# Two chunks' q loaded as token pairs behind the first raw weight blocks, and transposed by 64-column products

## Chip, core and metric

The kernel runs on one core of one Trainium2 chip. The metric is the device time of one execution in microseconds (us). The kernel before took 668.18, 668.00 and 666.48 us in three runs (median 668.0). Engines are named as in the profile: PE (TensorE, with PEld for its weight loads), DVE (VectorE), ACT (ScalarE), POOL (GpSimd) and SP (SyncE, which here only issues DMAs).

## What is computed

Attention with a decay over blocks of 64 tokens, then two dense layers with `h - tanh(h)` between them. Cut to what matters:

```python
# q, k, v: (batch 4, heads 8, tokens 768, head_dim 64) float32; lam: (8,)
Dmask = where(i >= j, lam ** (i - j), 0)
for b in range(12):                       # blocks of 64 tokens
    intra = (qb @ kb.T * Dmask) @ vb
    inter = (qb * lam ** (i + 1)) @ kv_state
    out[:, :, block] = intra + inter
    kv_state = lam ** 64 * kv_state + (kb * lam ** (63 - i)).T @ vb
x = out.transpose(0, 2, 1, 3).reshape(3072, 512)
h = x @ w_in                              # 512 x 2048
result = (h - tanh(h)) @ w_out            # 2048 x 512
```

The two weight matrices arrive as 8-byte floats (`moe_w_in`, `moe_w_out`), and the kernel rounds them itself.

## The kernel before

**Chunks and groups.** The kernel works on blocks of `BLK` = 128 tokens. A chunk is one such block of one batch entry with all 8 heads; a group `g` is the four chunks (`b` = 0 to 3) of the same block, so there are 6 groups. A chunk's q, k and v are each 128 tokens x 512 numbers, 256 KB. In the first two groups (`g < GB`) they are loaded with one token on a partition by `load_natural` (L127 to L133): 8 runs of 256 bytes on each of 128 partitions. Later groups load q and k in another form that the change does not touch.

**Attention of the first group.** `att_transpose` (L323) turns q and k of a chunk so that the head dimension lies on the partitions: four PE transposes of 128x128 into a PSUM bank `tp` (L336) and one ACT copy to SBUF (L338), first for q, then for k. A transposed tile has two heads stacked in its 128 partitions and four such pairs side by side. `att_scores` (L345) makes eight products `sp` of k and q (L352), and DVE multiplies them with the decay mask into `ss` (L356). `att_decay` (L361) scales k in place. `att_state` (L363) makes the state `kv` of two chunks (L374), which ACT copies to `state` (L382). `att_out` (L384) makes the output `op` of two chunks (L406), which ACT copies to `xt` (L410). Banks of the tag `att` come from a ring of four.

**First layer.** `up_plain(u, cs)` (L731) multiplies `xt` by unit `u` of `w_in` (L741), where a unit is a quarter of the 2048 columns and comes in four blocks of 512 KB. The first blocks are loaded with 128 partitions at once (L207), the third and fourth block of each unit in two halves of 64 partitions (L210). `round_block` rounds a raw block: three ACT passes (L289, L290, L291) and two DVE passes (L294, L296). Four raw buffers exist, so a fifth block's load waits until the first has been rounded. ACT's tanh (L748) and a DVE subtraction (L749) end `up_plain`.

**What sets the order.** The work of the first group is written out by hand and kept in program order on each engine (`tied`, `keep_in_program_order`): chunks 0 and 1 are transposed and scored one after the other, then `kv` of both; then chunk 2 is transposed, the first raw block rounded, `op` of chunks 0 and 1, scores of chunk 2, the first step of `up_plain(0, (11, 21))`, chunk 3's transposes and scores between the next steps, `kv` and `op` of chunks 2 and 3, and the last steps, of which the last two pairs need the third and the fourth raw block. Behind that come `up_plain(0, (12, 22))` and the next units. What is not tied is placed by a scheduler with its own estimates.

**Loads.** SP issues the opening loads in program order (L302 to L309): q, k, v of chunk 0, q, k, v of chunk 1, q and k of chunk 2, raw blocks 0 and 1, q and k of chunk 3, raw block 2 (two halves), v of chunks 2 and 3, raw block 3 (two halves). The q pool has two buffers, so the third q waits for the transposes of the first, and the fourth for those of the second. k has three buffers, so the fourth k waits for the `kv` products of chunk 0. The whole opening is SP's one queue.

Of the kernel before, what the change touches and what calls it, by code (L numbers as in the profile page):

```python
# [9 lines left out]
F32 = mybir.dt.float32  # L10
# [5 lines left out]
AF = mybir.ActivationFunctionType  # L16
AL = mybir.AluOpType

BLK = 128
GB = 2  # L20
# [4 lines left out]
def kernel(  # L25
# [32 lines left out]
    nc = tc.nc  # L58
    B, H, S, D = q.shape
    NTOK, DM = out.shape  # L60
    DFF = moe_w_in.shape[1]
    NP = H // 2
# [12 lines left out]
    io = ctx.enter_context(tc.tile_pool(name="io", bufs=4))  # L75
    work = ctx.enter_context(tc.tile_pool(name="work", bufs=2))
# [8 lines left out]
    qpool = early.enter_context(tc.tile_pool(name="qpool", bufs=2))  # L85
# [4 lines left out]
    ident = const.tile([128, 128], F32)  # L90
# [5 lines left out]
    for j in range(2):  # L96
        for p in range(NP):
            h = 2 * p + j
# [20 lines left out]
    def tied(yes, op):  # L119
        return tc.keep_in_program_order(op) if yes else op  # L120


    raw, late = {}, {}
    chunks = [(g, b) for g in range(NG) for b in range(B)]
    at = {"loaded": 0}

    def load_natural(g, b, names):  # L127
        for name, src, bufs in (("q", q, 2), ("k", k, 3), ("v", v, 4)):
            if name in names:
                x = (qpool if name == "q" else io).tile([128, H, D], F32, name=f"{name}_nat", tag=name, bufs=bufs)  # L130
                op = nc.sync.dma_start(out=x, in_=src[b, :, ts(g, BLK), :].rearrange("h s d -> s h d"))
                tc.keep_in_program_order(op)
                raw[g, b][name] = x  # L133
# [12 lines left out]
    def load(n):  # L146

        while at["loaded"] < min(n, len(chunks)):  # L150
            g, b = chunks[at["loaded"]]
            if g < GB:
                raw[g, b] = {}
                load_natural(g, b, "qkv")
                at["loaded"] += 1
                continue
            for b in range(B):
                raw[g, b] = {}
            nat = "kv" if g < NG - 1 else "v"

            first = (0, 1, 2) if g == GB else ()
            for b in first:
                load_natural(g, b, nat)
            for b in range(B - 1):
                load_blocks(g, b, "qk")
            load_blocks(g, 3, "q")
            for b in (0, 1):
                if b not in first:
                    load_natural(g, b, nat)
            load_blocks(g, 3, "k")  # L170
            for b in (2, 3):
                if b not in first:
                    load_natural(g, b, nat)
            at["loaded"] += B
# [27 lines left out]
    def load_block(eng, dst, kind, n, m, first=False):  # L202

        if kind == "out":
            tied(n > 4, eng.dma_start(out=dst, in_=moe_w_out[ts(2 * (n + m) - n % 2, 128), :].rearrange("k (a n) -> k a n", a=2)))
        elif m < 2:
            tied(first, eng.dma_start(out=dst, in_=w_in_u[ts(m, 128), n]))  # L207
        else:
            for j in range(2):
                tied(first, eng.dma_start(out=dst[ts(1 - j, 64)], in_=w_in_u[ts(2 * m + j, 64), n]))  # L210

    def load_weights(n):

        while ready["loaded"] < min(n, len(blocks)):
            if moe_w_in.dtype != F32:
                raw64 = stage.tile([128, 2, 256], I64, name="raw64", tag="raw64", bufs=WAHEAD)
                block = blocks[ready["loaded"]]
                load_block(nc.sync if block[0] == "in" or block[1] > 4 else nc.gpsimd, raw64, *block, block[0] == "in")
                wraw[ready["loaded"]] = raw64
            ready["loaded"] += 1  # L220
# [77 lines left out]
    def bank(name, tag, bufs):  # L298
        return psum.tile([128, 512], F32, name=name, tag=tag, bufs=bufs)


    for b in range(B):  # L302
        raw[0, b] = {}
        load_natural(0, b, "qkv" if b < 2 else "qk")
        if b >= 2:
            load_weights(b if b == 2 else 3)
    for b in (2, 3):
        load_natural(0, b, "v")
    load_weights(WAHEAD)  # L309
# [10 lines left out]

    tr, sc, kdec, xt = {}, {}, {}, {}

    def att_transpose(g, bs):  # L323
        for b in bs:
            load(g * B + b + 1)
            t = raw[g, b]
            qt = work.tile([128, NP, BLK], F32, name="qt", tag="qt")
            kt = work.tile([128, NP, BLK], F32, name="kt", tag="kt")
            for dst, x in ((qt, "q"), (kt, "k")):
                if g >= GB:  # L330
                    tc.keep_in_program_order(nc.vector.transpose(out=dst.rearrange("d p i -> d (p i)"),
                                                                 in_=t[x + "b"].rearrange("d p r a -> d (p r a)")))
                else:
                    tp = bank("tp", "att", 4).rearrange("d (p s) -> d p s", p=NP)
                    for p in range(NP):
                        tied(g == 0 or p == 0, nc.tensor.transpose(out=tp[:, p, :], in_=t[x][:, 2 * p:2 * p + 2, :],  # L336
                                                                   identity=ident))
                    tied(g == 0, nc.scalar.activation(dst, tp, AF.Copy))  # L338
            qd = None
            if g > 0:  # L340
                qd = work.tile([128, NP, BLK], F32, name="qd", tag="qd")
                nc.vector.tensor_tensor(qd, qt, fwd, op=AL.mult)
            tr[g, b] = (qt, kt, qd)
# [79 lines left out]
    def attention(g):  # L423
        pieces = [[(fn, g, bs) for fn in (att_transpose, att_scores, att_out, att_state)] for bs in ((0, 1), (2, 3))]
        pieces[1].append((att_sums, g, None))
        return pieces
# [378 lines left out]
    for b in (0, 1):  # L805
        att_transpose(0, (b,))
        att_decay(0, b)
        att_scores(0, (b,))
    att_state(0, (0, 1))
    half = up_plain(0, (11, 21))  # L810
    att_transpose(0, (2,))
    att_decay(0, 2)
    weights(1)
# [149 lines left out]
```

## Time and profile before

| What | Value |
|---|---|
| Median of three runs | 668.0 us (666.48 to 668.18) |
| Profiled execution, whole time | 667.48 us |
| Its span, first to last instruction | 665.7 us |
| PE busy | 653.7 us, 98% |
| DVE, ACT, POOL busy | 480.1, 214.8, 196.4 us |
| Granted PE clock | 1.00 in all stages |
| First 30 us: DMA engines | busy from 3 us on |

The span is the time from the first to the last instruction of one profiled execution; its whole time is 1.8 us longer. The views used below are: the page (busy times by engine), lists of waits (engine and line, what it waited for, us in total, times, longest), the chain of waits (followed back from the end, each step the thing that ended last), timelines (start, length, engine and line, tiles, count), a table of busy time by stage, and the DMA view, which gives for an issue the time until its data landed. PE instructions are counted as records; a product in this kernel shows as two records, a transpose as one. A busy PE is not PE at its peak, and records may be missing by a few per cent.

### The profile page before, as it was taken

Reading aid. Unit: us, or ns where it says so; the run is one execution under the profiler, and the core shown is the slowest. Engines: PE = TensorE matmul, PEld = TensorE weight load, DVE = VectorE, ACT = ScalarE, POOL = GpSimd, SP = SyncE. Lnnn points to the kernel's source line nnn. Section 1 sums busy time; section 2 is a strip of 40 time slices with the busy share of each in tenths; the row PEclk is TensorE's granted clock in tenths of the full one; section 3 lists DMA queues with packets and bytes.
Section 4 is the critical chain, followed back from the end, with each engine's and each line's share of the span. In section 5 each row is a group of like instructions: output and inputs, shape, how many; then the busy total and the mean of one; then the engine's idle time right before and its main releaser. Section 6 shows DMA issues by size and latency. Waiting matters only on the chain.

```text
span 665.7 us, 13244 instructions
## 1 busy us (share of the span) xinstructions
PE 653.7 (98%) x4992; PEld 594.6 (89%) x4992; DVE 480.1 (72%) x869; ACT 214.8 (32%) x413; POOL 196.4 (30%) x340
## 2 busy tenths in 40 slices
PE   8899999999999999999999999999999999999988
PEld 7788888888888999888999988999988899988987
DVE  4468897997778983489895378896378787357743
ACT  4788923423321113341112343112333112334110
POOL 0001415783122444001435101345200255300351
PEclk9999999999999999999999999999999999999999
DMA  9999936997345979426889533798721677600584
GB/s 215 226 205 272 294 124 221 347 323 215 79 91 147 294 219 268 88 52 133 233 236 288 132 73 87 182 291 252 202 50 37 156 239 237 205 16 1 141 278 167
DMA packets 158959, 121.76 MB, mean 183 GB/s; under 512 B 133872, under 2 KB 135024, under 8 KB 158896
## 3 DMA queue, kind: packets, MB, share of 16 engines
q0 software_dynamic: 26400, 86.27, 40.7%
q1 hardware_dynamic: 132352, 34.64, 25.6%
q8 instruction: 40, 0.66, 0.4%
q14 instruction: 23, 0.19, 0.1%
q10 hardware_dynamic: 144, 0.00, 0.0%
HBM read 100.67 MB, written 20.19 MB: 182 GB/s over the span
## 4 chain that ended last, share of the span: by engine, by line
PE 76%; issue 9%; DVE 5%; DMA 5%; POOL 2%; ACT 2%; SPq 1%; POOLq 0%; DVEq 0%; ACTq 0%
PE y L458 14%; PE y L686 11%; PE z L458 8%; PE zw L686 8%; PE h L741 7%; PE w L633 4%; PE y L633 4%; PE y L542 3%; PE sp L352 3%; PE op L406 3%; PE acc L771 2%; PE z L542 2%; PE op L400 1%; PE end L725 1%; DMA fine<-wt 1%
## 5 line engine op out<-in xcount | busy, mean ns | idle before, releaser
L598 POOL DMA_DIRECT2D wb<-fine x168 | 90.8, 540 | 138.0 <-PE y L686 59.8
L466 ACT ACTIVATE th<-g 128x512 f32<-128x512 f32 x76 | 47.6, 630 | 99.6 <-DVE g L471 34.2
L689 ACT ACTIVATE q<-y 128x128 f32<-128x128 f32 x96 | 26.7, 278 | 150.3 <-PE y L686 149.5
L458 PE MATMUL y<-xt,w 128*128 128x256 f32 x320 | 73.5, 380 | 0.0
L601 POOL DMA_DIRECT2D wb<-factors x44 | 23.9, 544 | 165.1 <-PE y L633 127.8
L458 PEld LDWEIGHTS y<-xt,w 128*128 128x128 f32 x320 | 59.9, 190 | 8.5 <-ACT g L546 0.9
L467 DVE TENSOR_TENSOR g<-g,th 128x512 f32<-128x512 f32 x76 | 52.1, 689 | 21.1 <-ACT th L466 21.0
L686 PE MATMUL y<-wb,g 128*128 128x128 f32 x456 | 60.6, 278 | 0.0
L741 PE MATMUL h<-xt,w 128*128 128x256 f32 x256 | 58.0, 383 | 1.5 <-DVE w L296 1.4
L686 PEld LDWEIGHTS y<-wb,g 128*128 128x128 f32 x456 | 55.1, 192 | 1.3 <-issue 0.3
L741 PEld LDWEIGHTS h<-xt,w 128*128 128x128 f32 x256 | 47.7, 190 | 9.4 <-DVE w L296 2.1
L686 PE MATMUL zw<-wb,g 128*128 128x128 f32 x304 | 40.3, 275 | 0.1
L458 PE MATMUL z<-tt,ws 128*128 128x256 f32 x160 | 38.1, 381 | 0.0
L458 PE MATMUL y<-tt,ws 128*128 128x256 f32 x160 | 37.8, 379 | 0.0
L458 PE MATMUL z<-xt,ws 128*128 128x256 f32 x160 | 37.8, 379 | 0.0
L686 PEld LDWEIGHTS zw<-wb,g 128*128 128x128 f32 x304 | 37.0, 192 | 0.2 <-DVE g L691 0.2
L633 PE MATMUL w<-wb,g 128*128 128x256 f32 x160 | 35.8, 382 | 0.0
L633 PE MATMUL y<-wb,g 128*128 128x256 f32 x160 | 35.4, 379 | 0.0
L356 DVE TENSOR_TENSOR ss<-sp,mask 128x512 f32<-128x512 f32 x48 | 31.1, 683 | 5.8 <-PE sp L352 5.8
L633 PEld LDWEIGHTS y<-wb,g 128*128 128x128 f32 x160 | 30.4, 190 | 4.1
L458 PEld LDWEIGHTS z<-xt,ws 128*128 128x128 f32 x160 | 30.4, 190 | 4.1
L633 PEld LDWEIGHTS w<-wb,g 128*128 128x128 f32 x160 | 30.1, 190 | 4.4
(178 smaller groups left out, 1292.9 us busy)
## 6 DMA issues: line engine op xcount, KB each, us to landing
wb<-fine POOLq DMA_DIRECT2D x168, 256.0 KB, 4.0
wb<-factors POOLq DMA_DIRECT2D x44, 256.0 KB, 4.3
v_nat<-in_v_dram SPq DMA_DIRECT2D x24, 256.0 KB, 4.8
wb<-fine_in POOLq DMA_DIRECT2D x24, 256.0 KB, 4.3
k_nat<-in_k_dram SPq DMA_DIRECT2D x20, 256.0 KB, 4.9
raw<-in_moe_w_out_dram POOLq DMA_DIRECT2D x10, 512.0 KB, 4.9
raw<-in_moe_w_in_dram SPq DMA_DIRECT2D x8, 512.0 KB, 5.7
raw<-in_moe_w_in_dram SPq DMA_DIRECT2D x16, 256.0 KB, 5.9
```

What stands on the lines that cost most here:

```text
L352: tied(g == 0, nc.tensor.matmul(out=sp[j][:, p, :], lhsT=kt[ts(j, 64), p, :], rhs=qt[ts(j, 64), p, :], start=True, stop=True))
L356: tied(g == 0, nc.vector.tensor_tensor(ss[:, j], sp[j], mask[:, j], op=AL.mult))
L458: nc.tensor.matmul(out=t[:, m, :], lhsT=wt[:, kt, ts(m, 128)], rhs=x[:, kt, :], start=first and m == 0 and kt == 0, stop=kt == 1, skip_gro ...
L466: nc.scalar.activation(th, src, AF.Tanh)
L467: nc.vector.tensor_tensor(dst(c), src, th, op=AL.subtract)
L542: nc.tensor.matmul(out=dst[:, ts(u, 128)], lhsT=a, rhs=b, start=x in (1, 2, 5) and u == 0, stop=True, skip_group_check=True)
L598: nc.gpsimd.dma_start(out=t.rearrange("p m c -> p (m c)"), in_=fine[TWICE.index(n_), SUB.index(x_)].rearrange("p u c -> p (u c)"))
L601: nc.gpsimd.dma_start(out=t, in_=factors[XAT[FACT[n_][1]]][:, 2 * x_:2 * x_ + 2, :])
L633: nc.tensor.matmul(out=t[:, m, :], lhsT=a[:, u, kt, ts(m, 128)], rhs=wb[:, kt, :], start=first and u == 0 and m == 0 and kt == 0, stop=u = ...
L686: nc.tensor.matmul(out=dst, lhsT=a[:, u, :], rhs=wb[:, ts(u, 128)], start=x in (1, 2) and u == 0, stop=u == NU - 1, skip_group_check=True)
L689: nc.scalar.activation(keep, dst, AF.Copy)
L741: tied(u == 0, nc.tensor.matmul(out=hm[c][:, m, :], lhsT=w1[u][:, i, a, ts(m, 128)], rhs=xt[0, t][:, i, :], start=m == 0 and i == 0, stop= ...
```

## The change

q of the first two groups now lies in tiles of two chunks (`qpair`, 1024 numbers on a partition, one buffer). Chunks 0 and 1 are loaded into the halves of such a tile as before. For chunks 2 and 3 of the first group the tile is filled by two loads of 64 partitions each, chunk 2 on partitions 0 to 63 and chunk 3 on 64 to 127: each partition holds two neighbouring tokens (`e` = 0, 1), so that a run in DRAM is 512 bytes. Both loads are issued behind raw blocks 0 and 1; the k of chunk 2 now comes right behind the v of chunk 1, and raw block 2 still follows the fourth k.

`att_queries`, called ahead of chunk 2's k transposes, turns both chunks at once: for each of the two token parities and each head a product of the 128x64 piece of q with the identity (16 in all, in place of eight transposes), two PSUM banks, and four ACT copies of 128x256, each of which writes every second column of chunk 2's or chunk 3's transposed tile. `att_transpose` of chunks 2 and 3 then transposes k alone.

For the second group q uses the same paired tiles, in the old form of loads and transposes; with one buffer, a pair's first load waits for both transposes of the pair before.

```diff
--- before.py
+++ after.py
@@ -120,14 +120,25 @@
         return tc.keep_in_program_order(op) if yes else op
 
 
-    raw, late = {}, {}
+    raw, late, qpair, qts = {}, {}, {}, {}
     chunks = [(g, b) for g in range(NG) for b in range(B)]
     at = {"loaded": 0}
 
     def load_natural(g, b, names):
-        for name, src, bufs in (("q", q, 2), ("k", k, 3), ("v", v, 4)):
+        if "q" in names:
+            if b % 2 == 0:
+                qpair[g, b // 2] = qpool.tile([128, 2 * H * D], F32, name="q_nat", tag="q", bufs=1)
+            x = qpair[g, b // 2]
+            for r in range(2) if (g, b) == (0, 2) else (b % 2,):
+                src = q[b - b % 2 + r, :, ts(g, BLK), :]
+                if g == 0 and b == 2:
+                    dst, src = x[ts(r, 64)], src.rearrange("h (t e) d -> t h e d", e=2)
+                else:
+                    dst, src = x[:, ts(r, H * D)], src.rearrange("h s d -> s h d")
+                tc.keep_in_program_order(nc.sync.dma_start(out=dst, in_=src))
+        for name, src, bufs in (("k", k, 3), ("v", v, 4)):
             if name in names:
-                x = (qpool if name == "q" else io).tile([128, H, D], F32, name=f"{name}_nat", tag=name, bufs=bufs)
+                x = io.tile([128, H, D], F32, name=f"{name}_nat", tag=name, bufs=bufs)
                 op = nc.sync.dma_start(out=x, in_=src[b, :, ts(g, BLK), :].rearrange("h s d -> s h d"))
                 tc.keep_in_program_order(op)
                 raw[g, b][name] = x
@@ -301,9 +312,11 @@
 
     for b in range(B):
         raw[0, b] = {}
-        load_natural(0, b, "qkv" if b < 2 else "qk")
-        if b >= 2:
-            load_weights(b if b == 2 else 3)
+        load_natural(0, b, "qkv" if b < 2 else "k")
+        if b == 2:
+            load_weights(2)
+            load_natural(0, 2, "q")
+    load_weights(3)
     for b in (2, 3):
         load_natural(0, b, "v")
     load_weights(WAHEAD)
@@ -320,13 +333,32 @@
 
     tr, sc, kdec, xt = {}, {}, {}, {}
 
+    def att_queries():
+
+        x = qpair[0, 1].rearrange("s (h e d) -> s h e d", h=H, e=2)
+        for r in range(2):
+            qts[2 + r] = work.tile([128, NP, BLK], F32, name="qt", tag="qt")
+        for e in range(2):
+            tp = bank("tp", "att", 4).rearrange("d (p s) -> d p s", p=NP)
+            for h in range(H):
+                tc.keep_in_program_order(nc.tensor.matmul(out=tp[ts(h % 2, 64), h // 2, :], lhsT=x[:, h, e, :],
+                                                          rhs=ident, start=True, stop=True))
+            for r in range(2):
+                dst = qts[2 + r].rearrange("d p (t e) -> d p e t", e=2)[:, :, e]
+                tc.keep_in_program_order(nc.scalar.activation(dst, tp[:, :, ts(r, 64)], AF.Copy))
+
     def att_transpose(g, bs):
         for b in bs:
             load(g * B + b + 1)
             t = raw[g, b]
-            qt = work.tile([128, NP, BLK], F32, name="qt", tag="qt")
+            if g == 0 and b == 2:
+                att_queries()
+            paired = g == 0 and b >= 2
+            if g < GB and not paired:
+                t["q"] = qpair[g, b // 2][:, ts(b % 2, H * D)].rearrange("s (h d) -> s h d", h=H)
+            qt = qts[b] if paired else work.tile([128, NP, BLK], F32, name="qt", tag="qt")
             kt = work.tile([128, NP, BLK], F32, name="kt", tag="kt")
-            for dst, x in ((qt, "q"), (kt, "k")):
+            for dst, x in ((qt, "q"), (kt, "k"))[paired:]:
                 if g >= GB:
                     tc.keep_in_program_order(nc.vector.transpose(out=dst.rearrange("d p i -> d (p i)"),
                                                                  in_=t[x + "b"].rearrange("d p r a -> d (p r a)")))
```

## Prediction

> **What bounds the kernel now.** The page first: it says which engine the span belongs to.
>
> ```profile
> PE 653.7 (98%) x4992; PEld 594.6 (89%) x4992; DVE 480.1 (72%) x869; ACT 214.8 (32%) x413; POOL 196.4 (30%) x340
> ```
>
> PE is idle for 12 us of 665.7. Next the list of PE's waits from 30 us to the end, to see which idle time lies behind the opening stage that the change touches:
>
> ```profile
> PE zw L686 <- DMA wb<-fine: 1.7, 1, 1.7
> PE h L741 <- DVE w L296: 0.9, 1, 0.9
> PE acc L771 <- DVE s L780: 0.8, 2, 0.7
> PE zw L686 <- DVE gS L691: 0.6, 1, 0.6
> ```
>
> That is all, 4.0 us. So from about 30 us PE never rests long, and whatever moves the start of that dense run moves the end of the kernel, but for what one of these four waits gives back. Now the chain of waits from 12 to 31 us, which tells what starts the dense run:
>
> ```profile
> 12.30 0.64 PE kv L374 x16
> ...
> 21.91 5.18 DMA raw<-in_moe_w_in_dram
> ...
> 29.16 0.70 DVE w L296
> 29.86 0.04 issue
> 29.91 1.13 PE h L741 x4
> ```
>
> The chain names a transfer: the fourth raw weight block lands at 27.08, ACT and DVE round it, and PE takes it at 29.91. PE's own timeline of that stretch shows that this is half of the truth (start, length, instruction, count):
>
> ```profile
> 12.23 1.15 PE L374 MATMUL kv<-v_nat,k_nat 128*64 128x64 f32 x32
> 13.31 0.66 PE L336 MATMUL tp<-ident,q_nat 128*128 128x128 f32 x4
> 13.81 0.60 PE L336 MATMUL tp<-ident,k_nat 128*128 128x128 f32 x4
> 14.34 1.97 PE L406 MATMUL op<-ss,v_nat 128*64 128x128 f32 x32
> 16.23 1.16 PE L352 MATMUL sp<-qt,kt 64*128 64x128 f32 x16
> 17.89 1.10 PE L741 MATMUL h<-xt,w 128*128 128x256 f32 x4 [0.49 <-DVE w L296]
> ```
>
> PE works from 13.31 with only two gaps (0.49 at 17.89, 1.14 at 20.57) and finishes what precedes that fourth block at 29.84 (eight instructions of h from 27.84). So two paths meet at 29.9, PE's own work and the transfer, and PE's has no slack: what delays its queue at 13.31 delays the dense run.
>
> **The change, part by part.** *Loads.* In the changed SP queue the third chunk's q is gone from its place ahead of the third k, and both q come as two 64-partition transfers behind the first two raw blocks. The two DMAs also wait for PE's transposes of the second q, which end at 9.73 (9.07 plus 0.66), before SP gets to them. How long until they land? SP's timeline has the issues, and the DMA view of each has its time to landing:
>
> ```profile
> 7.08 1.05 SPq L131 DMA_DIRECT2D q_nat<-in_q_dram  x1
> 8.17 1.14 SPq L131 DMA_DIRECT2D k_nat<-in_k_dram  x1
> 9.36 1.54 SPq L207 DMA_DIRECT2D raw<-in_moe_w_in_dram  x2
> 11.01 0.38 SPq L131 DMA_DIRECT2D q_nat<-in_q_dram  x1
> ```
>
> Third q: 7.08 + 5.0 = 12.1. Third k: 8.17 + 4.9 = 13.1. First raw block: 9.36 + 5.4 = 14.8; second, issued at 10.46, + 5.7 = 16.1. Fourth q: 11.01 + 6.3 = 17.3. Transfers land in the order of issue with no pause between them: a full queue, and the place in it sets the time. Without the third q (1.2 us) the second raw block lands at 14.9; then come the two halves. Their rate is not in the trace; the stage table (stretch, length, busy times, clock, DMA share, GB/s) bounds it:
>
> ```profile
> 4.00:11.00 7.00, 5.60 (x38) 4.09 (x36) 4.98 (x12) 2.30 (x4) 0.00 (x0) 1.00 1.24 223
> 13.00:14.50 1.50, 1.50 (x25) 1.27 (x23) 0.68 (x3) 1.02 (x2) 0.00 (x0) 1.00 0.95 377
> 28.50:31.00 2.50, 2.43 (x12) 1.82 (x11) 0.69 (x1) 2.05 (x5) 0.00 (x0) 1.00 1.02 182
> ```
>
> 4 to 11 us is q, k, v in 256-byte packets at 223 GB/s; 13 to 14.5 is mostly raw blocks in 4 KB packets over 128 partitions, 377; 28.5 to 31 is, by the count of packets before it, mostly raw halves of 64 partitions, 182. So 0.524 MB take 1.4 to 2.9 us. I take 2.3, the 223 GB/s of the nearest packet size: packets twice as long help, half the partitions hurt. The pair lands at **17.2** (16.3 to 17.8; later where one lagging engine holds the semaphore, as for the fourth k, issued at 12.96 and landed at 20.4, 3.1 behind the fourth q).
>
> [...]
>
> *The new wait.* In PE's changed queue the 16 products stand behind kv (ends 13.38) and wait for both halves. Queued behind them is everything: k's transposes, op, sp, h. PE idles from 13.4 to 17.2 where it now works.
>
> *From there to the dense run*, counted from the landing. 16 products of 128x64 weights on 128 columns have the form of op L406, 16 in 1.97, against 0.5 for four transposes. ACT then needs four copies of 128x256 instead of one of 128x512: between 128x128 (0.278, L689) and 128x512 (0.60) by length, 0.385 each, about 0.1 less back to back; with a step in the output perhaps 15% more (L290, which writes with a step, takes 0.787 against 0.679 for L289). The last two wait for the second eight products: copies end at +2.7, k's copy starts at +2.65, the first weight block at +3.1. In before it was +1.73 (15.04 from 13.31): 1.4 later, on the path, since h needs that block. From here spacings of before hold: h at +6.0 (2.85 behind the block), the second block's three ACT passes (1.8 each block) to +7.7, k's copy, sp at +8.4 (0.69 behind it), 1.1 of sp, 1.9 of h, 1.0 of kv, 1.85 of op, 2.0 of h: the dense run starts at **+16.25**. In before the same way took 16.6, with 1.14 of waiting for the fourth k and a q transpose and copy that are gone; k lands at 20.4 now and is not waited for any more. ACT has the fourth raw block rounded at +15.85 (landed long before), so PE sets it. 17.2 + 16.25 = 33.5 against 29.9: **+3.6**.
>
> *Given back.* At 67.18 PE waits 0.94 for the last weight block of the fourth unit, behind a saturated ACT. In the changed queues the second group's transposes stand four products earlier and a w_out pass (0.56) has moved behind that block on ACT; ACT's gap of 0.34 at 58.46 closes too. Together 0.9: the wait goes. Bounds: 0 and 0.94. I take -0.95 with rounding. Nothing else gives back: the DVE and DMA waits at 120, 227 and 637 us hang on work that PE's pace sets.
>
> *Costs nothing:* q of the second group now waits until both earlier chunks are transposed, some 0.9 later than the issue at 58.89; its transposes run at 82.57. POOL's first factor stores pass two w_out loads, in POOL's 2.58 of idle before 72.86.
>
> Sum: +3.6 - 0.95 = +2.65 on the profiled execution's 667.48 (span 665.7 and 1.8 around it), 0.5 under the median of the three runs, 668.0. Forecast **670.1**.
>
> **Rivals.** (a) *Less of a lag:* the pair moves at 377 GB/s, lands at 16.3, and the wait at 67 goes: +2.65 - 0.95 = +1.7, 669.2. For it: longer packets. Against: the 182 GB/s of half-width loads. (b) *Nothing is given back* at 67 us: +3.6, 671.1. For it: ACT's order there is dense and a late tanh could hold the block as before. (c) *PE turns slow after its rest.* In the first microseconds four transposes took 1.12, later 0.66, at a granted clock of 1.00 in the rows; if 3.8 idle us bring that back, the products and k's transposes take 1.7 times as long, about 1.8 more: 671.9. The longest rest of before is 1.7, so nothing shows it. [...] (d) *Faster:* the transfer path alone sets the dense run. The saved transfer time (2.35 down to 1.4) brings the fourth block 0.95 forward, and 0.95 comes back at 67: 665.6. It decides only if the pair lands before about 13.65, where PE's way still ends by 29.9; that needs q to pass the raw blocks in the queue, and every landing above is in order. That the change doesn't do what it says is ruled out by the queues as built: two 64-partition q loads, 16 products, four copies.
>
> **Chances.** Forecast 0.52, (a) 0.20, (b) 0.14, (c) 0.10, (d) 0.04. A measurement of this kernel tells about 0.3% (2.0 us) from no change. Slower by more: (b), (c) and all but 0.06 of the forecast, 0.70; within: 0.26; faster: 0.04. Range 668.4 to 672.5, from (a) with another 0.8 to (c) with a pair that lands 0.6 later; it leaves out (d).
>
> **What would show it.** PE idle from 13.4 to about 17.2 with the q pair as releaser; L344's 16 products in about 2; four copies at L348 ending about 2.7 behind the landing; the 65 products of the dense run starting near 33.5; no wait at about 70. It is wrong if the pair lands before 15, if PE has other work in that gap, or if a wait beyond 70 us shrinks with the lag.

## The result, and the profile after

The changed kernel took **675.22 us** (median of five runs, 674.12 to 676.27) against 668.0 for the kernel before: ratio 1.0114, interval 1.0096 to 1.0131. The forecast was 670.1 with a range up to 672.5. So the sign was right, the size was not: +7.7 us between the two profiled executions (675.22 against 667.48), where +2.65 had been worked out.

First the page of the changed kernel, for what hardly moved: PE's busy time.

```profile
span 673.4 us, 13292 instructions
PE 655.9 (97%) x5016; PEld 597.1 (89%) x5016; DVE 479.4 (71%) x869; ACT 214.8 (32%) x415; POOL 196.0 (29%) x340
```

PE is 2.2 us busier than before, and the span is 7.7 longer; so most of the loss is rest, and the 2.2 has to be looked for as well. The chain of waits of the changed kernel, in order of time (start, length, what), says where:

```profile
9.79 0.64 PE tp L368 x4
...
10.63 8.97 DMA q_nat<-in_q_dram
19.61 0.14 issue
19.74 3.68 PE tp L344 x32
23.43 1.06 PE tp L368 x4
...
27.00 0.70 DVE w L307
27.70 0.14 issue
27.84 1.10 PE h L773 x4
...
36.15 3.87 PE h L773 x17
```

Before, the step on the chain was a raw weight block. Now it is the second half of the pair: issued at 10.63, landed at 19.61. PE's timeline (start, length, instruction, count, idle before it) of the same stretch:

```profile
12.19 1.15 PE L406 MATMUL kv<-v_nat,k_nat 128*64 128x64 f32 x32
19.74 3.68 PE L344 MATMUL tp<-ident,q_nat 128*64 128x128 f32 x32 [6.40 <-DMA q_nat<-in_q_dram]
23.36 1.12 PE L368 MATMUL tp<-ident,k_nat 128*128 128x128 f32 x4
24.40 2.14 PE L438 MATMUL op<-ss,v_nat 128*64 128x128 f32 x32
...
34.23 1.92 PE L438 MATMUL op<-ss,v_nat 128*64 128x128 f32 x32
36.08 2.21 PE L773 MATMUL h<-xt,w 128*128 128x256 f32 x9
```

The rest ahead of the 16 products is there, with the releaser that was named, but it is 6.40 us and not 3.8. And the 16 products (32 records) take 3.68, where `op`, of the same form, takes 1.92 at 34.23. The eight instructions of h on the third block, at 27.84 before, start at 36.08: **8.24 later**. The line of the kernel before for them:

```profile
27.84 3.41 PE L741 MATMUL h<-xt,w 128*128 128x256 f32 x13
```

The table by stage has the reason for the 3.68 (stretch, length, busy times of PE, PEld, DVE, ACT, POOL, granted clock, DMA share, GB/s):

```profile
14.00:18.00 4.00, 0.00 (x0) 0.00 (x0) 0.00 (x0) 0.00 (x0) 0.00 (x0) 1.00 1.26 183
18.00:24.00 6.00, 4.26 (x35) 3.96 (x36) 0.00 (x0) 1.22 (x4) 0.00 (x0) 0.50 1.15 176
24.00:25.00 1.00, 1.00 (x11) 0.67 (x11) 0.49 (x1) 0.64 (x2) 0.00 (x0) 0.60 0.59 150
25.00:36.00 11.00, 10.79 (x146) 9.16 (x140) 6.86 (x13) 8.59 (x16) 0.00 (x0) 1.00 0.63 181
```

The granted clock falls to 0.50 at 18, while PE still rests, and is back before 25. The last column has the second clue: 183 GB/s from 14 to 18 us, where the kernel before moves 279 in the same four microseconds:

```profile
14.00:18.00 4.00, 3.51 (x53) 3.01 (x52) 2.07 (x4) 3.95 (x9) 0.00 (x0) 1.00 1.18 279
```

From 30 us to the end PE waits a little less than before, as its list of waits shows (us in total, times, longest):

```profile
PE y L718 <- DMA wb<-fine: 2.2, 3, 1.1
PE h L773 <- DVE g L781: 1.1, 1, 1.1
PE h L773 <- DVE w L307: 0.3, 1, 0.3
```

With the short ones 3.69 us against 4.16 before: 0.47 given back. 8.24 - 0.47 = 7.77 is, to 0.1, the difference of the spans (7.7). Nothing beyond 36 us is needed to account for the result; the rest of the study is about the 8.24.

### The profile page after: what moved, and what is told of

The parts are those of the page before. It is cut to its first block, busy times and chain, and to the rows that moved or that the text cites. A ratio compares the mean times of both kernels' runs of the same rounds, so it can differ in the third digit from the quotient of the medians.

```text
span 673.4 us, 13292 instructions
## 1 busy us (share of the span) xinstructions
PE 655.9 (97%) x5016; PEld 597.1 (89%) x5016; DVE 479.4 (71%) x869; ACT 214.8 (32%) x415; POOL 196.0 (29%) x340
## 4 chain that ended last, share of the span: by engine, by line
PE 66%; issue 15%; DMA 11%; POOL 4%; ACT 1%; DVE 1%; SPq 1%; POOLq 0%; DVEq 0%
PE y L490 12%; PE y L718 11%; PE z L490 8%; PE zw L718 8%; PE y L574 4%; PE w L665 4%; PE y L665 4%; PE h L773 3%; DMA wb<-fine 3%; PE sp L384 2%; PE z L574 2%; DMA fine<-f 2%; PE op L438 2%; DMA q_nat<-in_q_dram 1%; POOL wb L630 1%
## 5 line engine op out<-in xcount | busy, mean ns | idle before, releaser
L499 DVE TENSOR_TENSOR g<-g,th 128x512 f32<-128x512 f32 x76 | 52.1, 689 | 21.1 <-ACT th L498 21.0
```

What stands on the lines that cost most here:

```text
L499: nc.vector.tensor_tensor(dst(c), src, th, op=AL.subtract)
```

## The experiments

Three theories. **Landing:** the two 64-partition loads are slower than taken, and PE's whole queue stands behind them. **Clock:** the rest halves PE's clock, a loss of its own. **Form:** the 16 products and four copies cost more than eight transposes and two copies, wherever and whenever they run. The kernels ran in three sets, each beside the kernel before on the same chip (medians there 667.36, 666.72 and 667.52), so ratios are compared. "h3" stands for the start of h on the third block; it, the landings and the rest are those of the one profiled execution, and the ratio is that of all executions.

| Kernel | q landed (both loads) | rest of PE before it | h3 | ratio to before |
|---|---|---|---|---|
| before | 12.1, 17.3 | none | 27.84 | 1 |
| changed | 17.63, 19.61 | 6.40 | 36.08 | 1.0114 [1.0096, 1.0131] |
| e1_warm | 17.74, 19.40 | filled | 33.73 | 1.0058 [1.0038, 1.0078] |
| e2_old_form_late | 16.38, 17.59 | 3.10 | 30.76 | 1.0031 [1.0013, 1.0049] |
| e3_pair_early | 12.64, 14.04 | 0.72 | 28.66 | 1.0023 [1.0007, 1.0040] |
| e4_op_first | 17.96, 19.75 | 3.99 | 32.97 | 1.0079 [1.0058, 1.0101] |
| e5_full_width | 16.05, 17.11 | 2.85 | 32.40 | one execution, 673.11 us |
| e6_old_late_warm | 16.21, 17.33 | filled | 30.28 | 1.0043 [1.0016, 1.0071] |
| e7_full_width_warm | 16.61, 17.60 | filled | 31.41 | one execution, 668.94 us |
| e8_old_late_op_first | 16.27, 17.37 | 1.24 | 29.50 | 1.0017 [1.0001, 1.0034] |
| e9_half_old | 16.77, 19.53 | 3.59 | 31.14 | one execution, 671.34 us |
| e10_old_late_op_warm | 16.67, 17.61 | filled | 28.41 | 0.9988 [0.9969, 1.0007] |
| e11_op_first_warm | 17.71, 19.63 | filled | 31.52 | 1.0035 [1.0025, 1.0046] |

### e1_warm: the clock alone

```diff
+        for _ in range(22):
+            tc.keep_in_program_order(nc.tensor.matmul(out=idle[:, 0:128], lhsT=ident, rhs=ident, start=True, stop=True))
         x = qpair[0, 1].rearrange("s (h e d) -> s h e d", h=H, e=2)
```

> The changed kernel with 22 products of the identity put on PE ahead of the 16 q products, to fill its rest (13.3 to about 19.2) without touching a load. Theory (the pair lands late, and PE comes out of the rest at half clock): the pair still lands near 19.6, the clock stays 1.00, the 16 products take about 2.0 instead of 3.68, the dense run starts near 34.0 instead of 36.1, and the time is about 2.2 below the changed kernel, 673.0. Rival (the products and copies themselves are the cost, the clock is not): no difference, 675.2.

Measured: 671.74 us (673.0 expected), 0.56% below the changed kernel's ratio. Its PE timeline:

```profile
13.37 5.18 PE L339 MATMUL idle<-ident 128*128 128x128 f32 x44
19.53 1.97 PE L346 MATMUL tp<-ident,q_nat 128*64 128x128 f32 x32 [0.99 <-DMA q_nat<-in_q_dram]
...
33.73 3.50 PE L775 MATMUL h<-xt,w 128*128 128x256 f32 x15
```

The pair lands no earlier (19.40), yet h3 is 2.35 earlier: the products that do nothing keep the clock at 1.00, and the 16 that do take 1.97 rather than 3.68. The clock is a term of its own. The two profiled spans differ by more than that, 3.7; the other 1.4 is less waiting beyond 36 us (2.30 against 3.69). Most of it is the wait of 1.12 for DVE's `g` at 92.6, which is absent here, and no run ties that to the clock.

### e2_old_form_late and e3_pair_early: the place and the form apart

```diff
...
-        load_natural(0, b, "qkv" if b < 2 else "qk")
-        if b >= 2:
-            load_weights(b if b == 2 else 3)
+        load_natural(0, b, "qkv" if b < 2 else "k")
+        if b == 2:
+            load_weights(2)
...
+            load_natural(0, 2, "q")
+            load_natural(0, 3, "q")
+    load_weights(3)
```

> The kernel before with only the place changed: q of the third and fourth chunk in the old form (128 partitions, 256-byte runs, own transposes), both issued behind raw blocks 0 and 1. Theory (place in the queue and what it does to PE): the third q lands about 1.2 behind the second raw block, 16.2 to 17.6, PE rests 3 to 4 us, the dense run starts at 32 to 34.5, and the time is 670.5 to 672.5. Rival (the new form costs the time, the place nothing): 668.0 as before.

e2 keeps 128-partition loads of 256-byte runs and the transposes, and only moves both q behind the raw blocks. q lands at 16.38 and 17.59, PE rests 3.10, and the time is 669.13, less than the 670.5 to 672.5 expected. The clock falls after this smaller rest as well (granted 0.50 from 16.94 to 20.35): k's four transposes take 1.06 (0.60 before) and `op` 3.10 (1.97 before).

```profile
17.00 1.06 PE L340 MATMUL tp<-ident,k_nat 128*128 128x128 f32 x4
17.99 3.10 PE L410 MATMUL op<-ss,v_nat 128*64 128x128 f32 x32
```

The price of the place is 0.31%, that of the whole change 1.14%.

```diff
-            if b % 2 == 0:
+            if b % 2 == 0 and (g, b) != (0, 2):
                 qpair[g, b // 2] = qpool.tile([128, 2 * H * D], F32, name="q_nat", tag="q", bufs=1)
+            if g == 0 and b == 2:
+                qpair[g, 1] = wst.tile([128, 8, 256], F32, name="wt", tag="w").rearrange("p x c -> p (x c)")[:, 0:2 * H * D]
...
+        if b == 2:
+            load_natural(0, 2, "q")
         load_natural(0, b, "qkv" if b < 2 else "k")
         if b == 2:
             load_weights(2)
-            load_natural(0, 2, "q")
```

> The changed kernel with only the place undone: the pair in its new form, 16 products and four copies, but issued right behind the second chunk's v, ahead of the third k and the raw blocks (into a buffer that is free until later). Theory (place): the pair lands near 14, PE rests under 1 us at full clock, the dense run starts near 30.3, the time is 667 to 669. Rival (the form costs): products and copies add their time wherever they stand, 670 or more.

e3 has the changed form, issued right behind v of chunk 1 into a free buffer. The pair is there at 14.04, PE rests 0.72, the products take 1.97, and h3 is 0.82 later than before: that is all the form costs PE's opening. What it costs behind that is the transfer path: raw block 3 lands at 28.56 (27.08 before), and PE waits 0.72 for it at 31.38. The time, 669.31, lies between the two branches, and the profiled execution, the slowest of ten, has 2.2 us more of waits beyond 36 us than the kernel before, which no run explains. So the form by itself costs 0.23%, not 1.14%: the loss needs both, the slow loads *and* the place at which PE's queue meets them.

### e5_full_width and e7_full_width_warm: the width of the loads

```diff
-                    dst, src = x[ts(r, 64)], src.rearrange("h (t e) d -> t h e d", e=2)
+                    dst = x[:, ts(r, H * D)]
+                    src = q[b, ts(r, H // 2), 0:2 * BLK, :].rearrange("h (t e) d -> t h e d", e=2)
```

> The changed kernel with the pair's two loads over all 128 partitions with half the heads each, in 512-byte runs and with the same bytes; the rows come from the third chunk's batch entry alone (tokens 0 to 255), so the fourth chunk is computed from other tokens. Theory (64 partitions halve the rate): the pair moves at 280 GB/s or more, lands about 1.2 to 1.6 earlier, near 18.2, and the dense run starts as much earlier. Rival (512-byte runs set the rate): 174 to 192 GB/s in the stage and a landing near 19.6.

Same bytes, same 512-byte runs, same place, same products; the partitions differ, and with them the rows that are read (256 tokens of one batch entry in place of 128 of two). The pair lands at 17.11, a microsecond earlier than expected. The table by stage, from the landing of raw block 0 to that of the pair, first of the changed kernel:

```profile
13.80:19.60 5.80, 0.00 (x0) 0.00 (x0) 0.00 (x0) 0.19 (x1) 0.00 (x0) 0.86 1.22 188
```

and of e5_full_width:

```profile
13.40:17.10 3.70, 0.66 (x8) 0.45 (x8) 0.18 (x1) 0.58 (x1) 0.00 (x0) 1.00 1.22 291
```

Both stretches move about 1.08 MB (raw block 1 and the pair). The DMA engines are equally busy (share 1.22) and move 188 GB/s where the pair goes to 64 partitions at a time, 291 where it goes to all 128. Among the packets that the trace records, the 512-byte ones have a median of 51 ns at half width (46 to 53 in e1, e4 and e11, with the same loads) and 27 at full (27 in e7 too). And raw block 1, itself 128 partitions wide, lands at 16.41 against 15.15. The pair's packets start at 13.23, long before that block has landed, so that they share the engines with it; that this is why it lands later is argued, not shown by itself.

On top of e5:

```diff
+        for _ in range(12):
+            tc.keep_in_program_order(nc.tensor.matmul(out=idle[:, 0:128], lhsT=ident, rhs=ident, start=True, stop=True))
```

> e5_full_width (the changed kernel with the pair loaded over all 128 partitions, 512-byte rows from the third chunk's batch entry alone, so that the fourth chunk is computed from other tokens) with 12 products of the identity by itself ahead of the 16 products. Theory (what the changed kernel loses is the slow half-width load and the half clock, and nothing else of size): the pair lands near 17.1, the 16 products take 1.97 rather than 2.58, the third block's h starts near 30.5 to 31.3 rather than 32.40, and the span falls from 671.3 to some 669 to 670. Rival (the two costs overlap, so that only one of them counts): that h stays at 32.4 and the span at 671.3.

With both remedies h3 is at 31.41, beside the 31.45 that the prediction's sum has for it (17.2 + 16.25, less 2.0 for these eight instructions). The closeness is in part luck: the pair lands at 17.60, 0.40 later than in the sum, and the way from there is 0.44 shorter, as four of the 16 products need the first load alone and run before the second has landed. The span is 667.1, lower than either branch said, in part since PE waits only 2.7 us beyond 30 us in this execution.

### e9_half_old: is it the width or the rows?

On top of e2:

```diff
...
+                for r in range(2) if (g, name) == (0, "q") and b >= 2 else (None,):
+                    op = nc.sync.dma_start(out=x if r is None else x[ts(r, 64)],
+                                           in_=rows if r is None else rows[ts(r, 64)])
...
```

> e2_old_form_late with its two loads of q each cut into two loads of 64 partitions, the old form of 256-byte rows kept. Theory (a load onto half of the partitions runs at half the rate, whatever its rows): these rows take about 40 ns a packet, against 22 on 128 partitions, and the second q, which landed at 17.59, lands near 20; the third block's h starts near 33. Rival (the slow packets of the pair come from its 512-byte rows): 22 ns a packet, and q lands where it did, 16.4 and 17.6.

The theory fell in its own number: 256-byte packets onto 64 partitions take 26 ns (median from 14 to 17 us), not 40; on 128 partitions, in e2 and the same stretch, 19 (18 to 22 in e6, e8 and e10, with the same loads as e2). h3 is at 31.14, not near 33. Put together with e5 the four cases are:

| Packet | 128 partitions | 64 partitions |
|---|---|---|
| 256 bytes | 19 ns (e2) | 26 ns (e9) |
| 512 bytes | 27 ns (e5) | 51 ns (changed) |

At half width both sizes come out at 10 bytes per ns and packet (256/26, 512/51); at full width the longer packet moves more, 19 against 13. So in these runs the 256-byte packets take about a fifth to two fifths longer at half width, by which of e2, e6, e8 and e10 one compares with, and the 512-byte ones lose there all that their length brings at full width. The flow of e9 is not far behind e2's: 2,048 packets of 256 bytes, as many as the two q have, had started by 16.0 us in e2 and by 16.4 in e9. Still the last of e9's q lands at 19.53, 1.94 behind e2's: a tail behind the bulk that the packet times do not explain. It stays open, and with it how much of the changed kernel's landing is such a tail.

### e4_op_first and e11_op_first_warm: what stands behind the wait

```diff
-            if g == 0 and b == 2:
-                att_queries()
...
+    att_queries()
+    tr[0, 2] = (qts[2],) + tr[0, 2][1:]
     att_scores(0, (2,))
```

> The changed kernel with the op products of the first output block (and what goes ahead of them) put ahead of the 16 products on the pair; everything else, the loads too, as in the changed kernel. Theory (the loss is the wait at the head of TensorE's queue, plus the half clock that follows the rest): op and the transposes of k now run while the pair is on its way, so that some 2.0 us less is queued behind it; the rest shrinks from 6.40 to about 4.3 us, the clock falls all the same, and the third block's h starts near 34.0 rather than 36.08: about 673.0 to 673.5. Rival (the loss is in the 16 products and their copies, which cost what they cost wherever op stands): the start of that h and the time stay, 36 us and 675.

The changed kernel with `op` of chunks 0 and 1, k's transposes and the rounding of the first raw block ahead of the products: h3 at 32.97 (forecast 34.0) and 671.75, both lower than the theory had them. The rest is 3.99, and the clock falls at 21.1, when most of the 16 products are through (2.58 us for them).

On top of e4:

```diff
+    for _ in range(16):
+        tc.keep_in_program_order(nc.tensor.matmul(out=idle[:, 0:128], lhsT=ident, rhs=ident, start=True, stop=True))
     att_queries()
```

> e4_op_first (the changed kernel with op ahead of the 16 products) with 16 products of the identity by itself in the rest of 3.99 us ahead of the 16 products. What is left of the change is then the late pair itself. Theory (half clock and queue order are separate terms): the 16 products take 1.97, the third chunk's sp 1.16, and the third block's h starts near 31.6 rather than 32.97; about 670.3 against 671.75. Rival (with op out of the way the clock no longer sits on the path): that h near 32.5 and 671.5.

h3 31.52 (31.6 expected), 669.69 (670.3 expected). With loads exactly as slow as the changed kernel's, two edits of PE's queue bring its ratio from 1.0114 to 1.0035.

### e6, e8, e10: the old form at the late place, mended

> The kernel before with the two old loads of q moved behind the first two raw blocks, and 12 products of the identity by itself put into TensorE's rest ahead of the third chunk's transposes (e2_old_form_late without them: rest 3.10 us, transposes of k 1.06, op 3.10 at half clock, third block's h at 30.76, 669.13). Theory (a rest of 3 us is enough to halve the clock): the transposes of k take about 0.5, op about 1.9, that h starts near 29.2, and the time is about 667.7. Rival (the clock is an accident of that one execution and the load's lateness is all): as e2_old_form_late, h at 30.7 and 669.1.

(e2 with the same loop of 12 products ahead of chunk 2's transposes.) `op` takes 1.97 and k's transposes 0.60 as expected, but h3 is at 30.28, not 29.2, and the time is e2's. But in this execution the clock was at half earlier, from 7.74 to 11.16 us: the `sp` of chunk 0 takes 1.96 (1.16 in e2) and `kv` starts at 13.13 (12.26 in e2). So the 12 products start later too and last until 17.0, 0.5 beyond the point where e2 starts the transposes, and h then waits at 21.53 for the converted weights.

```profile
7.57 1.96 PE L356 MATMUL sp<-qt,kt 64*128 64x128 f32 x16 [0.69 <-ACT kt L342]
...
17.00 0.60 PE L340 MATMUL tp<-ident,q_nat 128*128 128x128 f32 x4
17.44 0.60 PE L340 MATMUL tp<-ident,k_nat 128*128 128x128 f32 x4
17.97 1.97 PE L410 MATMUL op<-ss,v_nat 128*64 128x128 f32 x32
19.86 1.16 PE L356 MATMUL sp<-qt,kt 64*128 64x128 f32 x16
21.53 1.10 PE L745 MATMUL h<-xt,w 128*128 128x256 f32 x4 [0.50 <-DVE w L296]
```

By the time the rival was right (ratio 1.0043 against e2's 1.0031), and the three of five executions with a mean clock of 0.999 or more (667.26, 668.79, 670.60) are no better. Why a kept clock buys nothing here is argued: h waits for weights whose conversion got its start from the same late q (ACT's first weight pass starts at 18.67, at 18.65 in e2). What h3 would be without the early half clock, no run shows.

On top of e2:

```diff
-    att_transpose(0, (2,))
-    att_decay(0, 2)
     weights(1)
     att_out(0, (0, 1))
+    att_transpose(0, (2,))
+    att_decay(0, 2)
```

> The kernel before with the two old loads of q moved behind the first two raw blocks and op of the first output block put ahead of the third chunk's transposes. Theory (what is queued behind the late q is the loss): op fills the rest, which falls from 3.10 to about 1 us; the clock stays up; the third block's h starts near 28 to 29, against 27.84 in the kernel before, while raw block 1 lands some 1.3 us earlier than there: 667 to 668, level with the kernel before or a little ahead of it. Rival (the opening is bound by the loads as a whole, so that one order of TensorE's work is as good as another): 669, as e2_old_form_late.

With `op` the rounding of the first raw block (`weights(1)`) goes ahead as well. h3 29.50 (28 to 29 expected), 667.76, ratio 1.0017: the time as the theory had it, but the clock falls even here. The table by stage:

```profile
16.00:18.00 2.00, 1.06 (x8) 0.86 (x8) 1.13 (x2) 1.71 (x4) 0.00 (x0) 1.00 1.15 217
18.00:21.00 3.00, 2.73 (x18) 2.42 (x19) 0.81 (x3) 2.05 (x4) 0.00 (x0) 0.51 1.02 198
```

No rest in it is longer than 1.24 us. This holds for the profiled execution; the mean clock was 0.997 in six of e8's twelve executions and at least 0.999 in the other six.

On top of e8:

```diff
     att_out(0, (0, 1))
+    for _ in range(5):
+        tc.keep_in_program_order(nc.tensor.matmul(out=idle[:, 0:128], lhsT=ident, rhs=ident, start=True, stop=True))
     att_transpose(0, (2,))
```

> e8_old_late_op_first with 5 products of the identity by itself between op and the third chunk's transposes, in the rest of 1.24 us that was left there. In e8 the clock was at half from 18.0 to 21.4, where the third chunk's sp took 2.08 and the first h 1.70 (1.16 and 1.13 at full speed). Theory (even this short rest, with the 0.80 behind it, costs the clock): full clock throughout, the third block's h starts near 28.2 rather than 29.50, and the time is about 1 us less than e8's: 666.5 to 667, level with the kernel before. Rival (the opening is held by the transfers and the conversion of the weights by then, as in e6_old_late_warm, where the full clock brought 0.5 us at that h and nothing in the time): that h near 29, 667.5 to 668.

Full clock in all twelve executions (0.999 or more), h3 at 28.41 (28.2 expected), 666.65 us, ratio 0.9988 with an interval of 0.9969 to 1.0007: level with the kernel before. q behind the raw blocks can be had for nothing, but no version that was tried is faster than the kernel before by more than its interval.

## Why the prediction was wrong, step by step

- **What bounds the kernel**: right. PE's own way sets the dense run, and what delays its queue at 13.3 delays the end; 8.24 at h3 came out as 7.7 in the span.
- **Landing of the pair, 17.2: the step that failed first.** "I take 2.3, the 223 GB/s of the nearest packet size: packets twice as long help, half the partitions hurt." It landed at 19.61, **2.41 later**. The row that was nearest in the property that counts was the other one: 182 GB/s for the raw halves of 64 partitions; 188 was measured. But even that end of the range (2.9 us for the pair) gave only 17.8, since the sum let raw block 1 land at 14.9 and began the pair behind it. In fact the pair's packets start at 13.23 and run beside that block, which lands at 16.41. The first packet of the pair is 4.8 us ahead of its last, at 18.06 (2.9 in e5_full_width), and the landing follows 1.5 behind that (0.8 in e5). "Transfers land in the order of issue" was right (raw blocks 0 and 1 at 13.8 and 16.41, the pair at 17.63 and 19.61); "with no pause between them" hid that they share the engines. That one lagging DMA engine holds a landing back, which the prediction names beside its range, was not shown: no view tells the engines apart. What half the partitions cost these 512-byte runs the traces do show: 188 GB/s over the stretch against 291 in e5, 51 ns against 27 for the same packet. "Packets twice as long help, half the partitions hurt" let the two make up for each other; with the half width the length brought nothing, 10 bytes per ns at 512 bytes as at 256.
- **The new wait and what stands behind it**: right in place and releaser, and e4 and e11 show what the order of the queue adds.
- **From the landing to h3**: forecast +14.25 (+16.25 less the 2.0 of its eight instructions), measured +16.47, that is **+2.22**. All of it is lost before the first h (at 27.84 in the changed kernel, +8.23 against +6.0); from there to h3 it takes 8.24, and 8.25 by the forecast. At full clock, in e1, the same way takes 33.73 - 19.40 = 14.33. So the working by rows held to 0.1 us (the copies as well: 0.68 for two, 0.67 taken), and the term that was missing is rival (c), the half clock, which had a chance of 0.10 and a price of 1.8.
- **Rival (c)'s weight.** The chance of 0.10 was the mistake. "The longest rest of before is 1.7, so nothing shows it" was no ground against it, since a rest of 3.8 had not been seen either way. Even with the landing as forecast the rest would have been 3.8, and in e2, e5 and e9 rests of 2.85 to 3.59 were each followed by half clock. What half clock costs stood in the trace of the kernel before, though the rows hide it: its record of the clock starts only at 7.16 us, and the rows (and the 1.00 in all stages) count the time ahead of that as full. The transposes that took 1.12 lie ahead of the record's start, those of 0.66 behind it; in the changed kernel, where the record starts at 4.31 with 1.00, the same first transposes take 0.66, and four of k take 1.12 at a granted 0.50, at 23.36. So that the first 1.12 was half clock is argued, as the record does not reach back to it. That a rest of 3.8 brings it back was not to be seen there.
- **Given back**: 0.95 taken, 0.47 measured. The wait of 0.94 shrinks to 0.25, and a new one of 1.12 for DVE at 92.6 us takes up most of what else had gone. Which edit makes that one was not tried.
- Sum: 2.65 + 2.41 + 2.22 + 0.48 = 7.76, against 7.74 measured.
- **Rivals**: (a) and (d) needed an earlier pair and fell with it; (b), nothing given back, was half true; (c) happened, on top of a later landing.

## What to carry to other kernels

When a load moves, ask first on how many partitions it lands and which other loads are in flight with it. Here the row for the same width, 182 GB/s, was nearer to the 188 measured than the 223 of the nearest packet size, and raw block 1, ahead of the pair in the queue, landed at 16.41 with the half-width pair and at 15.15 with the full-width one. The wait put at the head of PE's queue cost its length, 6.40 us, and also what PE's clock did around it, 0.50 for 6.83 us; filling the rest alone (e1) brought h3 2.35 forward. So put ready work ahead of such a wait (e4 has h3 3.11 earlier), and price half clock where PE may rest for 2.2 us or more out of 3.4, as it did ahead of five of the falls here (others came with less, see below). In the changed kernel, order and clock together (e11, ratio 1.0035) brought back more than the wider loads alone (e5, one execution, 673.11 against 675.22).

## What the runs showed of the hardware

By the granted clock in the traces, the half clock lasts 3.41 us in e2 (16.94 to 20.35), e4 (21.08 to 24.49), e5 (17.45 to 20.87), e6 (7.74 to 11.16), e8 (18.05 to 21.47) and e9 (16.89 to 20.30), and 6.83, twice that, in the changed kernel (17.96 to 24.79), whose full clock ahead of it lasts 13.65, four times that (4.31 to 17.96). So the traces are read here in stretches of 3.41 us, counted from these edges. The rows of e8 for the stretch ahead of its fall and the one at half clock:

```profile
14.64:18.05 3.41, 1.59 (x18) 1.14 (x14) 1.66 (x3) 3.12 (x6) 0.00 (x0) 1.00 1.23 222
18.05:21.47 3.42, 3.20 (x19) 2.80 (x20) 1.23 (x3) 2.00 (x4) 0.00 (x0) 0.50 1.07 201
```

and of the changed kernel, the empty one and the one that follows:

```profile
14.54:17.96 3.42, 0.00 (x0) 0.00 (x0) 0.00 (x0) 0.00 (x0) 0.00 (x0) 1.00 1.26 179
17.96:21.37 3.41, 1.63 (x16) 1.66 (x18) 0.00 (x0) 0.00 (x0) 0.00 (x0) 0.50 1.16 188
21.37:24.79 3.42, 3.42 (x28) 2.76 (x26) 0.28 (x1) 1.64 (x5) 0.00 (x0) 0.50 1.00 149
```

PE was busy for 1.59 of 3.41 us in the stretch ahead of e8's fall; for 0 (changed, e9), 0.43 (e2), 0.96 (e5) and 1.20 (e4) in the others. The stretch behind which the changed kernel stayed slow for a second turn had 1.63. But a stretch of e4 with 1.63 (14.26 to 17.67) was followed by none, nor was one of the kernel before with 1.71, while e6's early fall came behind one with 1.97:

```profile
635.22:638.63 3.41, 1.71 (x15) 1.54 (x15) 0.12 (x1) 0.28 (x1) 0.90 (x2) 1.00 0.94 330
4.33:7.74 3.41, 1.97 (x14) 1.30 (x15) 2.91 (x9) 1.20 (x2) 0.00 (x0) 1.00 1.21 226
```

So all five stretches with at most 1.20 were followed by half clock, and between 1.6 and 2.0 the busy time of the profile doesn't tell; what decides there, no run settles. Nor does the clock fall in every execution of a kernel: by the mean of each it fell in all five of the changed kernel (0.994 to 0.995), eight of ten of e2 (0.994 to 0.997), three of four of e4 (0.997), and none of e1, e10 and e11 (0.999 or more). The edges lie at other times in each profiled execution (17.96 in the changed kernel, 16.94 in e2); that this makes the difference between executions is argued, not shown.
